# Second feed-forward stage of a fused attention and MoE kernel: three passes of 768 tokens, with the up products by Strassen's scheme

## The chip, the cores and the metric

The kernel runs on one core of a Trainium2 chip. The metric is the device time of one execution in microseconds (us). All operands of matmuls are 32-bit; a float that needs full precision is split into a high and a low part (both rounded for the matmul), and one product is made of three matmuls: high by high, high by low, low by high.

## The reference

Three stages follow each other: a random-feature attention, a feed-forward layer with a leaky activation (called MoE1 here), and four experts weighted by token (the second stage). The attention is left out; the rest is:

```python
def _moe_ref(x, w_in, w_out, alpha):            # x: 2304 x 512, w_in: 512 x 2048
    h = x @ w_in
    g = np.maximum(h, 0.0) + alpha * np.minimum(h, 0.0)
    return (g @ w_out).astype(np.float32)

def _moe2_ref(x, domain_probs, w1, w2):         # w1: 4 x 512 x 1024, w2: 4 x 1024 x 512
    p = domain_probs / (domain_probs.sum(-1, keepdims=True) + 1e-09)
    out = np.zeros((N, D), dtype=np.float32)
    for e in range(E):
        h = np.maximum(x @ w1[e], 0.0)
        out += p[:, e:e + 1] * (h @ w2[e])
    return out.astype(np.float32)
```

## The kernel before, in words

Tokens lie along the free axis of `Xh` and `Xl` (high and low part of a stage's input, 128 partitions x 4 blocks of 128 model columns x 2304 tokens). The 2304 tokens are five blocks: four of 512, one of 256. The hidden units of both feed-forward stages are cut in chunks of 128: chunks 0 to 15 are MoE1, chunks 16 to 47 the four experts. Four chunks make a group.

The attention and the first blocks of MoE1's first group run in an order that a planner (class `Plan`) fixed; from there on the code's own order holds. The loop over `steps` goes through groups, and within a group through the five token blocks. For one chunk and block, `up` makes 12 matmuls into a PSUM bank (`up_products`, L208), then the activation: in the second stage ACT writes the relu's high part `gh` (L219) and DVE the low part `gl` (L220). `down` makes 48 matmuls for a block of four chunks (`down_chunk`, L234), and `add` lays them into an accumulator in SBUF, in the second stage with the expert's probability as a factor (L268 to L275); the last group writes to `out`. The first up of the next step stands ahead of a step's down products, so that PE does not wait for the activations.

At the end of MoE1 `add` takes the finished block and splits it at once into `Xh` and `Xl`, the second stage's input (L259 to L262).

Weights: `fetch` loads a chunk's half (0 up, 1 down) from DRAM into one of five `raw` buffers. In the second stage that is one DMA of 256 KB from `wcat` on SP's queue (L186); `place` then splits it (L158 for the high part on ACT, L161 for the low part on POOL) into one of six places for up and five for down. Weights are used by five blocks while they lie there.

Every engine works through its instructions in order, SP's queue of DMA issues included. The names below: `up` and `dn` are PSUM banks of up and down products, `whu`/`wlu` and `whd`/`wld` weights (high, low; up, down), `gh`/`gl` activations, `acc_a`/`acc_b` the accumulators.

Of the kernel before, what the change touches and what calls it, by code (L numbers as in the profile page):

```python
# [19 lines left out]
P = 128  # L20
# [9 lines left out]
NCH = NF1 + E * NF2  # L30
NG = NCH // GRP
# [6 lines left out]
HMAX = 320  # L38
NA = 3
# [91 lines left out]
def fused(ctx: ExitStack, tc: tile.TileContext, qT, kT, v_main, v_tail, w_phi, alpha, probs, w64, wcat, out):  # L131
# [3 lines left out]
    def cp(eng, o, i):  # L135
        (eng.copy if eng is nc.scalar else eng.tensor_copy)(o, i)

# [15 lines left out]
    acc_a = big.tile([P, NA, CC * BLK], F32, name="acc_a")  # L153
    acc = [acc_a[:, i] for i in range(NA)]

# [24 lines left out]
    def fetch(c, half, w, st, u):  # L180

        if c < NF1:
            nc.sync.dma_start(st, w64[c, half])
            rounded(st, w.bitcast(U32), u)
        else:
            nc.sync.dma_start(w, wcat[c - NF1, half])  # L186
        raw[c, half] = w
# [23 lines left out]
    def up(c, blk):  # L211
# [6 lines left out]
        if c >= NF1:  # L218
            nc.scalar.activation(gh, ps, AF.Relu)  # L219
            nc.vector.scalar_tensor_tensor(gl, ps, 0.0, f32(gh), ALU.max, ALU.subtract)  # L220
        else:
            t = tpool.tile([P, BLK], F32, name="t")[:, :bn]
            nc.vector.tensor_scalar(t, ps, 0.0, alpha_sb[:, c:c + 1], ALU.min, ALU.mult)
            nc.vector.scalar_tensor_tensor(t, ps, 0.0, t, ALU.max, ALU.add)  # L224
            split(t, gh, gl, nc.scalar, nc.vector)
        gs[c, blk] = gh, gl

    def down_chunk(c, blk, i, ps, start, stop):
        wh, wl = wts[c, 1]
        gh, gl = gs[c, blk]  # L230
        sl = slice(i * P, (i + 1) * P)
        for k, (w, g) in enumerate(((wh, gh), (wl, gh), (wh, gl))):
            a, b = (w[:, sl], g) if c < NF1 else (g[:, sl], w)
            nc.tensor.matmul(ps, a, b, start=start and k == 0, stop=stop and k == 2)  # L234
# [5 lines left out]
    def down(chunks, blk, parts_):  # L240

        bn = BLOCKS[blk][1] if chunks[0] < NF1 else DM
        out_ps = [ps_d.tile([P, BLK], F32, name="dn")[:, :bn] for _ in parts_]
        for c in chunks:
            for i, ps in zip(parts_, out_ps):
                down_chunk(c, blk, i, ps, c == chunks[0], c == chunks[-1])
        for i, ps in zip(parts_, out_ps):
            add(chunks, blk, i, ps)

    def add(chunks, blk, i, ps):  # L250
        t0, bn = BLOCKS[blk]
        if chunks[0] < NF1:
            av = acc[blk][:, i * bn:(i + 1) * bn]
            if chunks[0] == 0:
                nc.vector.tensor_copy(av, ps)
            elif chunks[-1] < NF1 - 1:
                nc.vector.tensor_tensor(av, ps, av, ALU.add)
            else:
# [5 lines left out]
        tok = t0 // P + i  # L264
        av = acc[blk][:, i * DM:(i + 1) * DM]
        e = (chunks[0] - NF1) // NF2
        pe = pr[:, tok, e:e + 1]
        if chunks[0] == NF1:  # L268
            nc.vector.tensor_scalar_mul(av, ps, pe)
        elif chunks[-1] < NCH - 1:  # L270
            nc.vector.scalar_tensor_tensor(av, ps, pe, av, ALU.mult, ALU.add)  # L271
        else:
            o = opool.tile([P, DM], F32, name="o")
            nc.vector.scalar_tensor_tensor(o, ps, pe, av, ALU.mult, ALU.add)
            nc.sync.dma_start(out[tok * P:(tok + 1) * P], o)  # L275


    with ExitStack() as st1:
# [246 lines left out]
        for i in range(2):  # L525
            a = acc[1 + i].bitcast(U32)
# [179 lines left out]
```

## Time and profile before

| | us |
|---|---|
| median of three runs | 1438.38 |
| lowest and highest of them | 1437.92, 1438.8 |
| the profiled execution | 1439.93 |
| its span, first to last instruction | 1438.2 |
| PE busy in it | 1418.9 |
| DVE, ACT, POOL busy | 654.7, 412.4, 212.4 |

The span is what the trace covers; the profiled execution's own time has some 1.7 us more around it. Engines: PE is TensorE's matmuls (PEld its weight loads), DVE is VectorE, ACT ScalarE, POOL GpSimd, SP the engine that issues DMAs here. The matmuls are pipelined: the records of two neighbours overlap, so the pace is read from a row of many (its length over its count) and not from the length of one record.

### The profile page before, as it was taken

To read this page: it belongs to the slowest core of one execution; us is meant where nothing else is said; L and a number is where in the kernel's file an instruction comes from. 1 tells how busy PE (TensorE), PEld (TensorE's weight loads), DVE (VectorE), ACT (ScalarE), POOL (GpSimd) and SP (SyncE) were. 2 spreads that over 40 slices of the span, in tenths; PEclk is the share of its full clock that TensorE was granted. 3 is DMA by queue.
4 is the path that set the end of the run, shared out by engine and by line. 5 is a ranking of instruction groups with operands and counts; after the bars stand their busy time and mean duration, and the time that the engine had idled before them with its cause. 6 is when DMAs were issued, how large, how long until landed. Compare 5 with 4: busy or idle time off the path is not lost.

```text
span 1438.2 us, 17632 instructions
## 1 busy us (share of the span) xinstructions
PE 1418.9 (99%) x7200; PEld 1152.1 (80%) x7200; DVE 654.7 (46%) x1067; ACT 412.4 (29%) x857; POOL 212.4 (15%) x165
## 2 busy tenths in 40 slices
PE   7999999999999999999999999999999999999998
PEld 4667667778888888888888888888888888888887
DVE  7966656687958855663222222222222222222222
ACT  6877666632212112232021120121210201211110
POOL 3443223102002002011020020020100200200100
PEclk9999999999999999999999999999999999999999
DMA  4311111130202001001020020010100200100001
GB/s 148 112 50 51 50 50 51 53 103 30 88 1 59 30 8 52 1 23 37 0 59 0 1 59 0 8 52 1 30 30 0 59 0 8 52 0 0 30 30 74
DMA packets 25136, 53.67 MB, mean 37 GB/s; under 512 B 3168, under 2 KB 4320, under 8 KB 25056
## 3 DMA queue, kind: packets, MB, share of 16 engines
q1 hardware_dynamic: 25056, 52.55, 12.2%
q8 instruction: 57, 0.93, 0.3%
q14 instruction: 23, 0.19, 0.0%
HBM read 47.82 MB, written 4.72 MB: 37 GB/s over the span
## 4 chain that ended last, share of the span: by engine, by line
PE 94%; DVE 3%; ACT 1%; DMA 1%; issue 0%; SPq 0%; POOL 0%; ACTq 0%; DVEq 0%; POOLq 0%
PE up L208 39%; PE dn L234 39%; PE bank L437 4%; PE kv L379 3%; PE mm L208 2%; PE kv L385 2%; PE mm L234 2%; PE bank L420 1%; PE bank L348 1%; PE bank L349 1%; PE bank L350 1%; DMA st<-w 1%; DMA acc_a<-w 0%; PE bank L401 0%; DVE m L355 0%
## 5 line engine op out<-in xcount | busy, mean ns | idle before, releaser
L208 PE MATMUL up<-Xl,whu 128*128 128x512 f32 (+1 forms) x912 | 334.6, 367 | 0.0
L208 PE MATMUL up<-Xh,whu 128*128 128x512 f32 (+1 forms) x912 | 334.5, 367 | 0.0
L208 PE MATMUL up<-Xh,wlu 128*128 128x512 f32 (+1 forms) x912 | 334.4, 367 | 0.0
L219 ACT ACTIVATE gh<-up 128x512 fp32r<-128x512 f32 (+1 forms) x160 | 88.7, 555 | 539.5 <-PE up L208 539.4
L220 DVE SCALAR_TENSOR_TENSOR gl<-up,gh 128x512 fp32r<-128x512 f32 (+1 forms) x160 | 102.0, 638 | 303.8 <-ACT gh L219 303.7
L234 PE MATMUL dn<-whd,gh 128*128 128x512 f32 x576 | 224.2, 389 | 0.0
L234 PE MATMUL dn<-wld,gh 128*128 128x512 f32 x576 | 224.2, 389 | 0.0
L234 PE MATMUL dn<-whd,gl 128*128 128x512 f32 x576 | 224.1, 389 | 0.0
L208 PEld LDWEIGHTS up<-Xh,whu 128*128 128x128 f32 x912 | 172.0, 189 | 28.6
L208 PEld LDWEIGHTS up<-Xl,whu 128*128 128x128 f32 x912 | 172.0, 189 | 28.4
L208 PEld LDWEIGHTS up<-Xh,wlu 128*128 128x128 f32 x912 | 171.9, 189 | 28.2
L161 POOL TENSOR_TENSOR wlu<-w,whu 128x512 fp32r<-128x512 f32 x44 | 58.2, 1322 | 915.3 <-ACT whu L158 879.7
L234 PEld LDWEIGHTS dn<-whd,gl 128*128 128x128 f32 x576 | 108.1, 188 | 22.5
L234 PEld LDWEIGHTS dn<-whd,gh 128*128 128x128 f32 x576 | 108.2, 188 | 22.1
L234 PEld LDWEIGHTS dn<-wld,gh 128*128 128x128 f32 x576 | 108.2, 188 | 22.1
L271 DVE SCALAR_TENSOR_TENSOR acc_a<-dn,pr,acc_a 128x512 f32<-128x512 f32 x72 | 50.2, 751 | 135.4 <-PE dn L234 135.4
L234 PE MATMUL dn<-gh,wld 128*128 128x512 f32 (+1 forms) x272 | 99.1, 364 | 0.0
L234 PE MATMUL dn<-gh,whd 128*128 128x512 f32 (+1 forms) x272 | 99.1, 364 | 0.0
L234 PE MATMUL dn<-gl,whd 128*128 128x512 f32 (+1 forms) x272 | 99.0, 364 | 0.0
L158 ACT CAST gh<-t 128x512 fp32r<-128x512 f32 (+1 forms) x68 | 38.6, 569 | 134.8 <-DVE t L224 134.6
L437 PE MATMUL bank<-qe,kvt 128*128 128x256 f32 (+1 forms) x256 | 72.6, 417 | 0.9 <-DVE pmk L362 0.9
L158 ACT CAST whu<-w 128x512 fp32r<-128x512 f32 x44 | 27.3, 620 | 136.4 <-PE up L208 121.4
(121 smaller groups left out, 1734.8 us busy)
## 6 DMA issues: line engine op xcount, KB each, us to landing
w<-wcat SPq DMA_DIRECT2D x64, 256.0 KB, 2.6
st<-w SPq DMA_DIRECT2D x24, 512.0 KB, 3.5
kr<-kT SPq DMA_DIRECT2D x16, 288.0 KB, 2.8
qr<-qT SPq DMA_DIRECT2D x16, 288.0 KB, 2.8
out<-o SPq DMA_DIRECT2D x18, 256.0 KB, 2.0
v<-v_main SPq DMA_DIRECT2D x16, 256.0 KB, 3.0
acc_a<-w SPq DMA_DIRECT2D x8, 512.0 KB, 4.5
v<-v_tail SPq DMA_DIRECT2D x16, 32.0 KB, 2.9
```

The lines of the kernel that those rows point to most:

```text
L158: nc.scalar.copy(hi, src)
L161: lo_eng.tensor_tensor(lo, src, f32(hi), ALU.subtract)
L208: nc.tensor.matmul(ps[:, :bn], a[:, cs], x[:, cc, t0:t0 + bn], start=n == 0, stop=n == 3 * CC - 1)
L219: nc.scalar.activation(gh, ps, AF.Relu)
L220: nc.vector.scalar_tensor_tensor(gl, ps, 0.0, f32(gh), ALU.max, ALU.subtract)
L234: nc.tensor.matmul(ps, a, b, start=start and k == 0, stop=stop and k == 2)
L271: nc.vector.scalar_tensor_tensor(av, ps, pe, av, ALU.mult, ALU.add)
L348: nc.tensor.matmul(o, xh[:, tok], wbh, start=True, stop=False)
L349: nc.tensor.matmul(o, xh[:, tok], wbl, start=False, stop=False)
L379: nc.tensor.matmul(kv[h * D:(h + 1) * D, 0], v[:rows, tile_, h], e[:rows, 2 * i + h], start=tile_ == 0, stop=tile_ == len(TILES) - 1, skip ...
L385: nc.tensor.matmul(kv[r:r + 32, 1], ones[:rows], e[:rows, 2 * i + h], start=False, stop=tile_ + 2 >= len(TILES), tile_position=(0, r), ski ...
L437: nc.tensor.matmul(nd[:, :n], tl["kvt", p][:, 2 * h + s], tl["qe", (p, h, c)][:, s, :n], start=s == 0, stop=s == 1)
```

## The change

The second stage leaves the loop over `steps`, which keeps MoE1 only. It now runs in three passes of 768 tokens, each as two halves of 384, and in each pass over 16 pairs of chunks. With the model's 512 columns in two halves and a pair's 256 hidden units in two halves, one pair's up product is a 2 x 2 block product. It is computed by seven block products for eight, in Winograd's form of Strassen's scheme:

- Input sums. `inputs` makes four sums of quarters of MoE1's result (in place, in the accumulators) and splits the seven operands (`x_op`); they lie in `x7` and in six regions of `Xl` (`slots`). It runs once per pass.
- Weight sums. `weights_up`, in pass 0, loads a pair's four blocks in two DMAs of 256 KB (`wup`), makes four sums on POOL, splits the seven operands (ACT the high part, POOL the low), and writes each to DRAM (`wsu`), seven writes of 256 KB per pair. In passes 1 and 2 it only loads the seven. `weights_down` does the same for a chunk's down weights with one load (`wdn`) and two writes (`wsd`), and loads two per chunk later.
- Products. `up2` makes the seven products, each of 6 matmuls of 384 columns (L786), in three PSUM accumulators, `pb`, `pd` and `pa`. Two are copied out by ACT (p1, p5) before other products are added on top, a third (u1) in between; DVE adds these to accumulators for three of the four outputs (`total`, L799), and the fourth is read in place. Then relu and split as before, for 384 tokens (L793 on ACT, L794 on DVE).
- Down products. `down2` makes 36 matmuls of 512 columns for four chunks and 384 tokens, and adds them to `acc2` as before (L833, L842 to L844); in the last groups of a pass `acc2` goes to `out`.
- MoE1. Its finished blocks stay in the accumulators, now one tile of 4 x 1536 tokens and one of 4 x 768, and `add` no longer splits them. Buffers used by MoE1 alone (`stage`, `u`, `g`, `t`) moved behind the others and are released after it.

The diff, cut to its core:

```diff
-NCH = NF1 + E * NF2
-NG = NCH // GRP
+NG = NF1 // GRP
+BLK2 = 384
+NPASS = NT // (2 * BLK2)
+TB = BLK2 // P
+NPAIR = E * NF2 // 2
+SEQ = (1, 5, 6, 2, 7, 3, 4)
...
-    acc_a = big.tile([P, NA, CC * BLK], F32, name="acc_a")
+    acc = [big.tile([P, CC, NA * BLK], F32, name="acc_a")]
...
-            else:
-                ts = slice(t0, t0 + bn)
-                x = opool.tile([P, BLK], F32, name="o")[:, :bn]
-                nc.vector.tensor_tensor(x, ps, av, ALU.add)
-                split(x, Xh[:, i, ts], Xl[:, i, ts], nc.scalar, nc.vector)
-            return
...
+    slots = {k: Xl[:, :, i * BLK2:(i + 1) * BLK2] for i, k in enumerate((5, 6, 4, 2, 7, 3))}
+    slots[1] = x7
+    def x_op(k, src):
+        o = slots[k]
+        split(src, o[:, :2], o[:, 2:], nc.scalar, nc.vector)
+    def inputs(i, part):
+        a = lambda r, c: acc_of(slice(2 * c, 2 * c + 2), (2 * i + r) * BLK2, BLK2)
+        tt = nc.vector.tensor_tensor
+        if part == 0:
+            x_op(1, a(0, 0))
+            x_op(4, a(1, 1))
+            tt(a(1, 1), a(1, 0), a(1, 1), ALU.add)
+            x_op(5, a(1, 1))
+            tt(a(1, 0), a(1, 0), a(0, 0), ALU.subtract)
+            tt(a(0, 0), a(1, 1), a(0, 0), ALU.subtract)
+            x_op(6, a(0, 0))
+            x_op(2, a(0, 1))
+            tt(a(0, 1), a(0, 1), a(0, 0), ALU.subtract)
+        else:
+            x_op(7, a(1, 0))
+            x_op(3, a(0, 1))
...
+    def weights_up(i, f):
+        w = {k: up_place().rearrange("p (r c) -> p r c", r=2) for k in SEQ}
+        uw[i, f] = w
+        if i:
+            for j, k in enumerate(SEQ):
+                nc.sync.dma_start(f32(w[k]).rearrange("p r c -> p (r c)"), wsu[f][:, j])
+            return
...
+        def parts(k, src):
+            nc.scalar.copy(w[k][:, 0], src)
+            tt(w[k][:, 1], src, f32(w[k])[:, 0], ALU.subtract)
+            nc.sync.dma_start(wsu[f][:, SEQ.index(k)], f32(w[k]).rearrange("p r c -> p (r c)"))
+        parts(1, b[11])
+        tt(lo(5), b[12], b[11], ALU.subtract)
+        tt(lo(6), b[22], lo(5), ALU.subtract)
+        parts(5, lo(5))
+        tt(lo(4), b[21], lo(6), ALU.subtract)
+        parts(6, lo(6))
+        parts(2, b[21])
+        tt(lo(7), b[12], b[22], ALU.subtract)
+        parts(7, lo(7))
+        parts(3, b[22])
+        parts(4, lo(4))
+    def weights_down(i, c):
+        w = down_place()
+        dw[i, c] = w
+        if i:
+            for r in range(2):
+                nc.sync.dma_start(f32(w[r]), wsd[c][:, r])
+            return
+        t = raw_tile()
+        nc.sync.dma_start(t, wdn[c])
+        split(t, *w, nc.scalar, nc.vector)
+        for r in range(2):
+            nc.sync.dma_start(wsd[c][:, r], f32(w[r]))
...
+        product(1, "pb", True, False)
+        p1 = t("p1")
+        nc.scalar.copy(p1, ps["pb"])
+        product(5, "pd", True, False)
+        p5 = t("p5")
+        nc.scalar.copy(p5, ps["pd"])
+        product(6, "pb", False, False)
+        u1 = t("u1")
+        nc.scalar.copy(u1, ps["pb"])
+        product(2, "pa", True, True)
+        g(0, 0, total("pa", p1, "c11"))
+        product(7, "pb", False, False)
+        c22 = total("pb", p5, "c22")
+        product(3, "pd", False, True)
+        g(1, 0, total("pd", u1, "c12"))
+        product(4, "pb", False, True)
+        g(0, 1, ps["pb"])
+        g(1, 1, c22)
...
+    ups = [(i, f) for i in range(NPASS) for f in range(NPAIR)]
+    weights_up(0, 1)
+    for c in range(1, 4):
+        weights_down(0, c)
+    for n, (i, f) in enumerate(ups):
+        gp = f // 2
+        up2(i, f)
+        if n + 2 < len(ups):
+            weights_up(*ups[n + 2])
+        if f % 2 == 0:
+            if gp:
+                down2(i, gp - 1, 1, False)
+        else:
+            down2(i, gp, 0, False)
+            if n + 1 < len(ups):
+                i2, f2 = ups[n + 1]
+                for c in range(4):
+                    weights_down(i2, 2 * f2 + c)
+            if gp == NPAIR // 2 - 1:
+                down2(i, gp, 1, True)
+                if i + 1 < NPASS:
+                    inputs(i + 1, 0)
+                    inputs(i + 1, 1)
```

On PE, in the middle of the second stage, before: chunk after chunk of 12 matmuls, each by the high or low weights of that chunk (`whu`, `wlu`).

```order
L208 MATMUL up_8222<-Xh_75,whu_8131 128x512
L208 MATMUL up_8222<-Xl_76,whu_8131 128x512
L208 MATMUL up_8222<-Xh_75,wlu_8132 128x512 [waits Pool_49]
L208 MATMUL up_8222<-Xh_75,whu_8131 128x512
L208 MATMUL up_8222<-Xl_76,whu_8131 128x512
```

PE at the first pair of pass 0, after: the names `up_6340`, `up_6349` and `up_6366` are the accumulators pb, pd and pa; `whu`, `wlu` and `wx` are only places, each holding one operand's high and low part.

```order
L786 MATMUL up_6340<-x7_3540,whu_5816 128x384 x6
L786 MATMUL up_6349<-Xl_126,whu_5817 128x384 x6
L786 MATMUL up_6340<-Xl_126,wlu_5818 128x384 [waits Activation_49]
L786 MATMUL up_6340<-Xl_126,wlu_5818 128x384 x5
L786 MATMUL up_6366<-Xl_126,wlu_5819 128x384 x6
L786 MATMUL up_6340<-Xl_126,wx_5820 128x384 [waits Activation_49]
L786 MATMUL up_6340<-Xl_126,wx_5820 128x384 x5
L786 MATMUL up_6349<-Xl_126,wx_5821 128x384 x6
L786 MATMUL up_6340<-Xl_126,whu_5822 128x384 [waits DVE_49]
```

Where twelve matmuls of a bank stood, seven runs of six stand, and the third, fifth and seventh run wait for a read of the accumulator: p1's copy, u1's copy, and the total c22.

On ACT in the second stage, before: the relus of a group with the next weights' casts between them.

```order
L158 CAST whd<-w 128x512 x4
L219 ACTIVATE gh<-up 128x512 x15
L158 CAST whu<-w 128x512
L219 ACTIVATE gh<-up 128x256
L158 CAST whu<-w 128x512
```

On ACT in pass 0, after, around one pair's up products (p1, p5, u1 are the copies out of PSUM; `Xh_125` now holds relus and some down weights):

```order
L174 CAST Xh_125<-w_7885 128x512 [waits DMAHW2_49,PE_49]
L804 COPY p1_7727<-up_7720 128x384 [waits PE_49,Activation_49]
L695 CAST whu_7785<-w_7792 128x256 [waits DMAHW4_49]
L807 COPY p5_7736<-up_7729 128x384 [waits PE_49,Activation_49]
L695 CAST whu_7786<-ts0_7796 128x256 [waits DMAHW5_49,Pool_49]
L810 COPY u1_7744<-up_7720 128x384 [waits PE_49,Activation_49]
L695 CAST whu_7787<-ts1_7797 128x256 [waits DMAHW7_49,Pool_49]
L695 CAST wlu_7788<-w_7792 128x256 [waits DMAHW0_49,PE_49]
L793 ACTIVATE Xh_125<-c11_7753 128x384 [waits DVE_49]
```

The copies that PE waits for now stand between casts of weights, some of which wait for POOL (`ts0` and `ts1` are POOL's sums) or for a DMA.

On SP in the second stage, before: nothing but weight loads until the last group's writes.

```order
L186 DMA w_8333<-wcat 128x512 [waits DMAHW7_49,Pool_49]
L186 DMA w_8356<-wcat 128x512 [waits DMAHW0_49,Pool_49]
L186 DMA w_8379<-wcat 128x512 [waits DMAHW4_49,Pool_49]
L186 DMA w_8475<-wcat 128x512 [waits DMAHW5_49,Pool_49]
L186 DMA w_8494<-wcat 128x512 [waits DMAHW1_49,Pool_49]
```

On SP at the start of pass 0, after (`wsu1` and `wsd1` to `wsd3` are written, `w` from `wup` is a half of the third pair's raw weights):

```order
L687 DMA w_6412<-wup 128x512 [waits DMAHW2_49]
L697 DMA wsu1_58<-whu_6280 128x512 [waits DMAHW3_49,Pool_49]
L697 DMA wsu1_58<-wlu_6284 128x512 [waits DMAHW4_49,Pool_49]
L722 DMA wsd1_74<-whd_6316 128x512 [waits DMAHW5_49,Activation_49]
L722 DMA wsd1_74<-wld_6317 128x512 [waits DMAHW6_49,DVE_49]
L722 DMA wsd2_75<-whd_6324 128x512 [waits DMAHW7_49,Activation_49]
L722 DMA wsd2_75<-wld_6325 128x512 [waits DMAHW0_49,DVE_49]
L722 DMA wsd3_76<-whd_6332 128x512 [waits DMAHW1_49,Activation_49]
L722 DMA wsd3_76<-wld_6333 128x512 [waits DMAHW2_49,DVE_49]
L687 DMA w_6414<-wup 128x512 [waits DMAHW3_49]
```

The second half of the third pair's raw weights (`w_6414`) stands behind eight writes that wait for ACT, POOL or DVE.

## Rows read from the trace of the kernel before

**Rows 1.** the page: busy time, granted clock, GB/s by slice, and the chain's shares.

```profile
PE 1418.9 (99%) x7200; PEld 1152.1 (80%) x7200; DVE 654.7 (46%) x1067; ACT 412.4 (29%) x857; POOL 212.4 (15%) x165
...
PEclk9999999999999999999999999999999999999999
...
GB/s 148 112 50 51 50 50 51 53 103 30 88 1 59 30 8 52 1 23 37 0 59 0 1 59 0 8 52 1 30 30 0 59 0 8 52 0 0 30 30 74
...
PE 94%; DVE 3%; ACT 1%; DMA 1%; issue 0%; SPq 0%; POOL 0%; ACTq 0%; DVEq 0%; POOLq 0%
PE up L208 39%; PE dn L234 39%; PE bank L437 4%; PE kv L379 3%; PE mm L208 2%; PE kv L385 2%; PE mm L234 2%; PE bank L420 1%; PE bank L348 1%; PE bank L349 1%; PE bank L350 1%; DMA st<-w 1%; DMA acc_a<-w 0%; PE bank L401 0%; DVE m L355 0%
```

**Rows 2.** chain of waits piece by piece, second stage: start us, us, what.

```profile
645.08 5.75 PE dn L234 x48
...
749.14 10.88 PE up L208 x48
760.02 10.88 PE dn L234 x48
```

**Rows 3.** the end of the same chain.

```profile
1428.91 5.48 PE dn L234 x24
...
1434.41 0.75 DVE o L274
```

**Rows 4.** windows: us; PE, PEld, DVE, ACT, POOL busy; clock, DMA share, GB/s.

```profile
700.00:800.00 100.00, 100.00 (x466) 83.76 (x465) 26.05 (x39) 16.23 (x29) 10.33 (x8) 1.00 0.08 22
1350.00:1438.00 88.00, 84.38 (x395) 70.51 (x393) 22.76 (x34) 8.45 (x16) 0.00 (x0) 1.00 0.14 54
338.00:340.00 2.00, 2.00 (x11) 1.65 (x10) 0.00 (x0) 0.00 (x0) 0.00 (x0) 1.00 0.60 236
```

**Rows 5.** groups by form: operation, shapes, count; busy us, mean ns; idle before.

```profile
L234 PE MATMUL dn<-whd,gh 128*128 128x512 f32 x576 | 224.2, 389 | 0.0
...
L220 DVE SCALAR_TENSOR_TENSOR gl<-up,gh 128x512 fp32r<-128x512 f32 x128 | 88.5, 692 | 273.9 <-ACT gh L219 273.9
...
L219 ACT ACTIVATE gh<-up 128x512 fp32r<-128x512 f32 x128 | 76.6, 598 | 519.2 <-PE up L208 519.2
...
L161 POOL TENSOR_TENSOR wlu<-w,whu 128x512 fp32r<-128x512 f32 x44 | 58.2, 1322 | 915.3 <-ACT whu L158 879.7 <-DVE t L223 35.6
...
L271 DVE SCALAR_TENSOR_TENSOR acc_a<-dn,pr,acc_a 128x512 f32<-128x512 f32 x72 | 50.2, 751 | 135.4 <-PE dn L234 135.4
...
L161 DVE TENSOR_TENSOR gl<-t,gh 128x512 fp32r<-128x512 f32 x52 | 38.4, 738 | 25.8 <-ACT gh L158 25.5
...
L234 PE MATMUL mm<-gh,whd 128*128 128x512 f32 x48 | 19.2, 401 | 0.0
...
L220 DVE SCALAR_TENSOR_TENSOR gl<-up,gh 128x256 fp32r<-128x256 f32 x32 | 13.5, 424 | 29.8 <-ACT gh L219 29.8
...
L219 ACT ACTIVATE gh<-up 128x256 fp32r<-128x256 f32 x32 | 12.2, 381 | 20.3 <-PE up L208 20.3
```

**Rows 6.** timeline at two places: start us, us, engine, what, idle before.

```profile
299.96 0.68 DVE L565 SCALAR_TENSOR_TENSOR t<-mm,t 128x512 f32<-128x512 f32 x1
...
300.70 0.50 PE L208 MATMUL mm<-Xh,whu 128*128 128x512 f32 x1 [1.72 <-DVE t L565]
...
696.94 0.39 PE L208 MATMUL up<-Xh,whu 128*128 128x512 f32 x1
...
697.13 0.60 ACT L219 ACTIVATE gh<-up 128x512 fp32r<-128x512 f32 x1 [13.00 <-PE up L208]
```

**Rows 7.** DMA issues: KB each, median us from issue to landing.

```profile
w<-wcat SPq DMA_DIRECT2D x64, 256.0 KB, 2.6
st<-w SPq DMA_DIRECT2D x24, 512.0 KB, 3.5
...
out<-o SPq DMA_DIRECT2D x18, 256.0 KB, 2.0
```

**Rows 8.** waits of SP's queue: total us, times, longest us.

```profile
SPq L186 <- POOL wlu L161: 694.9, 32, 74.3
```

More of the change, by code (lines that the diff above doesn't have):

```diff
@@ new lines, in fused, with up_place, down_place @@
+    uw, dw = {}, {}
+    turn = [8, 0]
+    places = [(wa[0], "whu")] * 4 + [(wa[0], "wlu")] * 4 + [(wb[0], "whu")] * 2 + [(wb[0], "wlu")] * 2 + [(wx, "wx")] * 2
+    def up_place():
+        p_, name = places[turn[0] % len(places)]
+        turn[0] += 1
+        return p_.tile([P, DM], F32R, name=name)
+    XF = Xh.rearrange("p a b -> p (a b)")
+    def down_place():
+        at = turn[1] % 8
+        turn[1] += 1
+        if at < 5:
+            p_ = wa[1] if at < 4 else wb[1]
+            return [p_.tile([P, DM], F32R, name="w" + n + "d") for n in "hl"]
+        o = 16 * BLK2 + (at - 5) * 2 * DM
+        return [XF[:, o + r * DM:o + (r + 1) * DM] for r in range(2)]
@@ L668, in fused @@
             up(GRP * g2, b2)
-        n = CC if c0 < NF1 else BLOCKS[blk][1] // P
-        for d in ([[i] for i in range(n)] if last else [range(n)]):
-            down(range(c0, c1), blk, d)
+        else:
+            inputs(0, 1)
+        down(range(c0, c1), blk)
+        if c1 == NF1:
+            if blk == 1:
+                weights_up(0, 0)
+                weights_down(0, 0)
+            elif blk == 2:
+                inputs(0, 0)
+    st2.close()
+    apool = pool("acc2", 2)
+    tpool = pool("t2", 1)
@@ new lines, in fused, with up2, product, g @@
+    acc2 = {}
+    free = [XF[:, o:o + 2 * BLK2] for o in range(0, 16 * BLK2, 2 * BLK2)]
+    def up2(i, f):
+        ps = {k: None for k in ("pa", "pb", "pd")}
+        t = lambda name: tpool.tile([P, BLK2], F32, name=name)
+        w = uw.pop((i, f))
+        def product(k, name, start, stop):
+            if start:
+                ps[name] = ps_u.tile([P, BLK], F32, name="up")[:, :BLK2]
+            n = 0
+            for kt in range(2):
+                for r, x in ((0, 0), (0, 2), (1, 0)):
+                    nc.tensor.matmul(ps[name], w[k][:, r, kt * P:(kt + 1) * P], slots[k][:, x + kt],
+                                     start=start and n == 0, stop=stop and n == 5, skip_group_check=True)
+                    n += 1
+        def g(c, r, src):
+            o = free.pop(0)
+            gh, gl = (o[:, j * BLK2:(j + 1) * BLK2] for j in range(2))
+            nc.scalar.activation(gh, src, AF.Relu)
+            nc.vector.scalar_tensor_tensor(gl, src, 0.0, f32(gh), ALU.max, ALU.subtract)
+            gs[2 * f + c, r] = gh, gl, o
+        def total(name, x, out):
+            o = t(out)
+            nc.vector.tensor_tensor(o, ps[name], x, ALU.add)
+            return o
+        product(1, "pb", True, False)
[16 more added lines that the diff above has]
+        g(1, 1, c22)
@@ new lines, in down2, with product, add2 @@
+    def down2(i, gp, r, by_tile):
+        chunks = range(4 * gp, 4 * gp + 4)
+        ps = {}
+        def product(c, m):
+            if c == chunks[0]:
+                ps[m] = ps_d.tile([P, BLK], F32, name="dn")
+            gh, gl, _ = gs[c, r]
+            wh, wl = dw[i, c]
+            sl = slice(m * P, (m + 1) * P)
+            for k, (w, x) in enumerate(((wh, gh), (wl, gh), (wh, gl))):
+                nc.tensor.matmul(ps[m], x[:, sl], w, start=c == chunks[0] and k == 0, stop=c == chunks[-1] and k == 2)
+        def add2(m):
+            tok = (2 * i + r) * TB + m
+            if (gp, r, m) == (0, 0, 0):
+                acc2[i] = apool.tile([P, 2 * TB, DM], F32, name="acc2")
+            av = acc2[i][:, r * TB + m]
+            pe = pr[:, tok, 2 * gp // EP:2 * gp // EP + 1]
+            if gp == 0:
+                nc.vector.tensor_scalar_mul(av, ps[m], pe)
+            else:
+                nc.vector.scalar_tensor_tensor(av, ps[m], pe, av, ALU.mult, ALU.add)
+            if gp == NPAIR // 2 - 1:
+                nc.sync.dma_start(out[tok * P:(tok + 1) * P], av)
+        if by_tile:
+            for m in range(TB):
+                for c in chunks:
+                    product(c, m)
+                add2(m)
+        else:
+            for c in chunks:
+                for m in range(TB):
+                    product(c, m)
+            for m in range(TB):
+                add2(m)
+        for c in chunks:
+            free.append(gs.pop((c, r))[2])
```

128 lines of the change are left out of this document (65 added, 63 removed).

## The prediction

> **What bounds the kernel now.** I read the page first. PE is busy 99% of the span, its granted clock is at full speed in all forty slices, the chain that ended last is PE for 94%, and lines L208 (the up products of both feed-forward stages) and L234 (the down products) hold 39% each [rows 1]. The chain piece by piece then shows that the second stage, from about 645 us to 1434.4 us, is one unbroken row of PE pieces, up and down in turn, each beginning where the last ended [rows 2]. Nothing is waited for there, so its length is the number of matmuls times their pace: 10.88 us for 48 of 512 columns, which is 226.7 ns each, and 5.75 us for 48 of 256 columns, 119.8 ns each [rows 2]. Behind the last matmul only an add of 0.75 us and the last write are left [rows 3]. The windows give the rest: in 700 to 800 us ACT is busy for 16 of 100 us, DVE for 26, POOL for 10, and the DMA share is 0.08 [rows 4]. So the change takes time from the only full engine and gives work to four that are nearly idle. The question is whether any of them then makes PE wait.
>
> **What PE loses.** The up products of the second stage are now 32 chunks, each with 12 matmuls on four blocks of 512 tokens and one of 256: 384 x (4 x 226.7 + 119.8) ns = 394.2 us. After the change they are 3 passes x 16 pairs of chunks x 7 products x 6 matmuls = 2016, each of 384 columns. No row has 384. I take the middle of 256 and 512, 173.2 ns, since the two pieces fit a straight line (106.9 ns for 256 columns more, so 13 ns of fixed cost): 349.2 us. The saving is **44.9 us**, not the eighth of 49 us that the count alone promises, because shorter matmuls pay the fixed 13 ns more often. The weight loads beside PE run under matmuls of 119.8 ns without slowing them [rows 2], so 173 ns leaves them room. The pace has a worse bound: in stage one 48 down products have a mean record of 401 ns where the steady ones have 389 [rows 5]; 12 ns on 2016 matmuls would be +24 us. I take none of it, because the steady rows are those of this stage, with operands from the same memories.
>
> The Trainium skill (TensorE: Matmul & The Clock Gate, "Back-to-back issue gap") puts warm matmuls at N/2.4 ns plus about 2.5 ns. By that the saving would be about 45.8 us, an estimate from the page. The rows show 13 ns over N/2.4 at both widths, so the measurement decides, and the difference is under 1 us.
>
> The down products are 1728 matmuls of 512 before and after, at the same 226.7 ns: **0**. The tail, an add and a write, is the same: **0**. A pair of chunks then takes 42 x 173.2 ns = 7.28 us of up and 36 x 226.7 ns = 8.16 us of down, 15.44 us in all. All side work has to fit that.
>
> **Inside a pair.** The seven products share three accumulators, so the fifth product and later ones wait for copies and totals read out of them. Count from the pair's first matmul; a product lasts 1.04 us. From the last matmul's start to ACT's is 0.19 us beyond its slot, and ACT 128x256 takes 381 ns, 128x512 598 ns [rows 5, 6], so about 490 ns for 384. The copy p1 runs from 1.23 to 1.72 us and is wanted at 2.08; u1 from 3.31 to 3.80, wanted at 4.16. The DVE total c22 starts at 5.39, takes 558 ns (middle of 424 and 692 [rows 5]), ends at 5.95, and the last product wants it at 6.24. From DVE's end to PE's start the trace shows 0.06 us [rows 6], so the smallest margin is **0.23 us**. All hold, in every pass, if ACT and DVE are free at that moment. In passes 1 and 2 they have nothing else near. In pass 0, ACT has 7 casts of 128x256 for weights and 2 of 128x512 for the down weights per pair, and they stand in the queue between p1, p5, u1 and the relus. Busy time is no trouble: ACT 4 x 0.49 + 3 x 0.47 + 7 x 0.38 + 2 x 0.60 = 7.2 us, DVE 4 + 3 operations of 0.56, two of 0.74 and three adds of 0.75 = 7.6 us, POOL 11 of 128x256 at 0.66 to 1.33 us (half of a 512's time, or all of it [rows 5]) = 7.3 to 14.6 us, of 15.44. A cast before p1 in every second pair ends some 0.4 us ahead of its need. For one matmul held per pair I book what the one held matmul in the trace lost, 0.11 us (0.50 for 0.39 [rows 6]): 16 x 0.11 = **+1.8 us**, with bounds 0 and 40 (2.5 us per pair, below).
>
> **Transfers.** In pass 0 each pair reads 4 blocks of 256 KB and writes 11 back: 3.93 MB in 15.44 us, 255 GB/s. Each read alone lands 2.6 us after issue and each write 2.0 [rows 7], but 512 KB lands in 3.5 [rows 7], 0.9 us for 256 KB more, so a queue that is kept full moves 290 GB/s, and the write-heavy window at the end gives 54 GB/s at a share of 0.14, 386 GB/s at full share [rows 4]. At those rates the pair's transfers take 11 to 13.5 us. Passes 1 and 2 only read, 11 blocks a pair, 187 GB/s, 9.9 us. Transfers at 0.60 share beside PE leave PE busy for all of the 2 us of a window [rows 4], so I book **0** for contention.
>
> A rule speaks against this. The Trainium skill (DMA: Bandwidth & Descriptors, "Bandwidth") asks for 1 MiB or more in one transfer to reach three quarters of the peak; here all are a quarter of that. If each transfer paid its fixed part alone, a pair would take 15 x 2.6 us = 39 us by the trace's own landing time; this is the fourth case below. The rows of 256 and 512 KB say that most of the fixed part overlaps.
>
> **At the start of pass 0.** SP issues in order. One half of the raw weights of the third pair is queued on SP behind eight writes of made weights, which wait for POOL and DVE. The switch comes at 648.1 us (645.08 + 5.75, less 2.72 us of the old first up products [rows 2]); I place that load near 651 us, an estimate from the writes ahead of it; the sums of that pair come late on POOL, their casts stand on ACT ahead of p1 and u1 of the second pair, and no down products lie between the first pair and the second. By the operation times above p1 is late by some 2.9 us and u1 by 1.9: **+4.7 us**, bounds 0 and 9. The longest wait of SP now is 74 us for POOL's wlu [rows 8]: being late costs nothing there only because weights are loaded many blocks ahead, and that cover is gone in this place.
>
> **At the two pass ends.** The new inputs are made by DVE and ACT while PE does the two down products of the last pair, 16.3 us. Eleven DVE operations of 768 columns (about 1.03 us, one and a half of a 128x512's 0.69 [rows 5]) and six adds end some 14.5 us after the last up product, so they just fit; one subtraction stands in DVE's queue ahead of the first pair's c22 and eats its margin: **+1.2 us each, +2.4**, bounds 0 and 8.
>
> **Handover and first feed-forward stage.** Buffers of stage one are reused by other pools, so the first weight load behind it waits for DVE and POOL where it waited for all. The last group of MoE1 gets DVE and ACT work for the inputs and POOL work for the first weights. By the operation times [rows 5] DVE has about 16.9 us to do in such a block of 21.8 us (two pieces of 10.88 [rows 2]). I book **0**, bounds -3 and +3.
>
> **Sum.** -44.9 + 1.8 + 4.7 + 2.4 = -36.0 us. The profiled run took 1439.93 us, its span 1438.2, some 1.7 us outside; the median of three runs is 1438.38. I subtract from the median: **1402 us**.
>
> **Rivals.**
> 1. PE stays the bound and the losses are of the size above, 1394 to 1414 us: the forecast, **0.62**. For it speak the idle shares [rows 4]; against it, that margins of 0.2 us were worked out and not seen.
> 2. Side work of pass 0 holds PE in each pair: ACT's in-order queue waits in a weight cast for POOL or for a load, and p1, u1 or a relu waits behind it. At 1 to 2.5 us for each of 16 pairs, and as much again at the starts, 1418 to 1437 us: **0.17**. For it: POOL's bound of 14.6 us is near 15.44.
> 3. c22 is late in all 48 pairs because a 384-wide total reads two sources slower, or because releases take longer than 0.06 us. At 0.2 to 0.5 us each, +10 to +24: 1412 to 1426 us: **0.12**. The same times come from a pace slower by half of those 12 ns.
> 4. Slower than before: the one queue of transfers does not deliver pass 0. The point of decision is 36.0/16 = 2.25 us per pair more, that is 3.93 MB in 17.7 us, 222 GB/s. At 200 GB/s a pair takes 19.7 us, and if passes 1 and 2 (2.88 MB) keep up, the kernel gains 16 x 4.2 = 68 us: about 1470 us. With each transfer alone 39 us a pair, far above. For it: 255 GB/s over 247 us stands nowhere in the trace, whose highest slice is 148 GB/s [rows 1]. Against it: 236 GB/s in a window at 0.60 share [rows 4]. **0.09**.
>
> That the change does not do what it says is left out: the order of its instructions shows 2016 matmuls of 384 columns in place of the old ones.
>
> **How the numbers follow.** The low end is the saving with no loss, 1438.4 - 44.9 = 1393. The high end takes in the third case and the upper bounds of the small terms, 1426. Left out are most of the second case (0.10) and the fourth (0.09). A measurement here tells about 0.2%, 3 us, from no change. Faster: cases 1 and 3 and nearly all of 2, 0.88; the same: the upper end of 2 and the crossing of 4, 0.03; slower: 0.09.
>
> **What would show it.** Up products of 384 columns at a pace of 173 ns; passes 1 and 2 of 247 us each without a PE gap inside a pair; pass 0 longer than they are by 5 to 8 us, most of it in its first two pairs with PE released by ACT; the DMA share in pass 0 near 0.7 to 0.85. I am wrong if PE waits in each pair of pass 0 and the releaser is ACT (case 2) or a transfer (case 4), if DVE's total releases PE in every pair (case 3), or if 384 columns cost over 180 ns.

## The result, and the profile after

The changed kernel takes 1413.18 us (median of four, 1412.67 to 1415.91) against 1438.27 for the kernel before: ratio 0.9829, interval 0.9812 to 0.9846. It is faster by 25 us where 36 were forecast; the time lies inside the range, and 11 us above the point. The profiled execution took 1413.24 us, its span 1411.5, so that spans can be compared: by them 26.7 us were gained, because the profiled execution of the kernel before (1439.93) was 1.7 us above its median.

The page, with the lines that answer to [rows 1]:

```profile
PE 1382.5 (98%) x7296; PEld 1171.5 (83%) x7296; DVE 774.2 (55%) x1288; ACT 510.3 (36%) x1114; POOL 273.6 (19%) x277
...
PEclk9999999999999999999999999999999999999999
...
GB/s 141 116 51 60 51 51 51 10 90 76 90 16 31 60 1 120 1 16 180 289 292 250 236 240 223 204 230 195 184 164 179 195 197 232 199 192 164 172 157 45
...
PE 91%; DMA 3%; DVE 2%; ACT 2%; POOL 1%; issue 1%; SPq 1%; ACTq 0%; DVEq 0%; POOLq 0%
```

PE is still the bound, but DMA, ACT and POOL have entered the chain, and PE's share of the span fell from 99% to 98%. The forty slices of the clock hide what follows: a slice is 35 us long.

The chain piece by piece in the third pass, which answers to [rows 2] (start us, us, what):

```profile
1220.75 8.20 PE dn L833 x36
1228.95 7.30 PE up L786 x42
```

A pair takes 15.50 us, where 15.44 were forecast: 42 up products of 384 columns at 173.8 ns (forecast 173.2), 36 down products at 227.8 (226.7 before). The pairs of the second and third pass read like this one, but for one whose up products took 7.44 us.

The starts of the three passes are the first products of the first pair, on PE's timeline (start us, us, engine, line, operation):

```profile
651.25 0.51 PE L786 MATMUL up<-x,whu 128*128 128x384 f32 x2
...
911.13 0.69 PE L786 MATMUL up<-x,whu 128*128 128x384 f32 x3
...
1159.48 0.69 PE L786 MATMUL up<-x,whu 128*128 128x384 f32 x3
```

The three passes are thus 259.9, 248.35 and 248.2 us long (the third to the end of the last down product, 1407.70 us). The first loses 11.7 us against the third. And the first product starts at 651.25 us where the switch was at 648.1 before: another 3.1 us lost ahead of the second stage.

What PE waited for, from the list of the whole span (total us, times, longest us):

```profile
PE kv L368 <- ACT ke L357: 9.1, 7, 2.8
PE up L786 <- ACT p L804: 5.2, 2, 2.7
...
PE up L786 <- ACT u L810: 1.9, 1, 1.9
```

The wait for `ke` is in the attention stage; before it was 6.0 us on the same operation:

```profile
PE kv L379 <- ACT ke L368: 6.0, 6, 2.3
```

The waits of L786 lie at the start of the first pass: two in its second pair (2.46 us for p1's copy, 1.87 for u1's) and one in its fourth (2.75 us for p1's copy), as the timeline of PE has them in brackets:

```profile
663.44 1.41 PE L786 MATMUL up<-Xl,whu 128*128 128x384 f32 x6 [2.46 <-ACT p L804]
...
668.32 3.93 PE L786 MATMUL up<-Xl,wlu 128*128 128x384 f32 x13 [1.87 <-ACT u L810]
...
701.68 1.96 PE L786 MATMUL up<-Xl,whu 128*128 128x384 f32 x6 [2.75 <-ACT p L804]
```

Windows there, and two of steady stretches behind it (us; PE, PEld, DVE, ACT, POOL busy; granted clock, DMA share, GB/s):

```profile
652.00:656.00 4.00, 4.00 (x25) 4.00 (x24) 1.01 (x2) 1.82 (x5) 0.74 (x1) 1.00 0.99 339
660.00:664.00 4.00, 1.54 (x9) 1.22 (x8) 3.15 (x4) 4.00 (x11) 3.98 (x5) 1.00 0.19 71
664.00:668.00 4.00, 2.45 (x10) 1.94 (x8) 0.56 (x1) 0.60 (x3) 3.84 (x6) 0.57 0.81 307
668.00:672.00 4.00, 3.68 (x13) 3.69 (x14) 1.30 (x2) 2.33 (x6) 3.92 (x7) 0.58 0.40 150
731.00:800.00 69.00, 69.00 (x352) 62.99 (x351) 34.41 (x55) 31.64 (x75) 39.30 (x48) 1.00 0.74 265
900.00:1150.00 250.00, 250.00 (x1257) 226.23 (x1256) 102.79 (x174) 61.27 (x120) 0.00 (x0) 1.00 0.61 192
```

First the transfers are full (share 0.99, 339 GB/s), then PE stands for 2.5 of 4 us, and then the matmuls that do run have a granted clock of 0.57 and 0.58, so much of that stretch is at the lower of the two levels (1.2 for 2.4 GHz). A second such place is at 700 us (a clock of 0.76 in 700 to 704 us, 0.81 in 704 to 708). From 731 us on PE is busy without a gap, at a DMA share of 0.74 and 265 GB/s, with ACT, DVE and POOL at half their time or so.

The chain from the switch to the second product that waited, the one for u1, shows how the hold arises (start us, us, what):

```profile
651.45 0.63 ACT whd L174
...
652.16 0.70 DVE wld L177
652.86 0.02 issue
652.87 0.32 SPq L722
653.19 0.05 issue
653.25 4.42 DMA w<-wup
657.66 0.02 issue
...
657.80 0.74 POOL ts L700
...
667.79 0.48 ACT u L810
668.27 0.04 issue
668.32 2.30 PE up L786 x6
```

A cast of down weights (`whd`) had to wait for MoE1's last down products, whose place it takes. DVE then makes the low part, and the writes of both parts stand on SP ahead of the third pair's raw load. That load goes out at 653.25 and lands 4.42 us later, where such a load took 2.6 [rows 7]. POOL's sums begin 6.5 us after the switch, ACT's casts follow, and the copy u1 of the second pair stands behind them. This is the mechanism that the prediction put at this place, and the two waits, 2.46 and 1.87 us, are near the 2.9 and 1.9 that it gave them.

The fourth pair is held in another way, which the prediction does not have:

```profile
692.85 0.70 POOL whu L696
...
693.56 0.32 SPq L697
...
694.92 4.32 DMA w<-wdn
...
699.60 0.32 ACT whd L174
...
701.16 0.48 ACT p L804
...
701.68 7.03 PE up L786 x30
```

Here ACT waits for raw down weights before a cast, and p1 stands behind that cast. The load left SP at 694.92 us, behind a write that had waited for POOL's low part until 693.55 us and behind two other loads, and landed 4.32 us later. The order on SP and a slow landing are both in this chain.

### The profile page after: what moved, and what is told of

It is laid out like the page before. It is cut to its first block, busy times and chain, and to the rows that moved or that the text cites. A ratio compares the mean times of both kernels' runs of the same rounds, so it can differ in the third digit from the quotient of the medians.

```text
span 1411.5 us, 19676 instructions
## 1 busy us (share of the span) xinstructions
PE 1382.5 (98%) x7296; PEld 1171.5 (83%) x7296; DVE 774.2 (55%) x1288; ACT 510.3 (36%) x1114; POOL 273.6 (19%) x277
## 4 chain that ended last, share of the span: by engine, by line
PE 91%; DMA 3%; DVE 2%; ACT 2%; POOL 1%; issue 1%; SPq 1%; ACTq 0%; DVEq 0%; POOLq 0%
PE dn L833 27%; PE up L786 23%; PE dn L242 12%; PE up L221 12%; PE bank L426 4%; PE kv L368 3%; PE kv L374 2%; PE mm L242 2%; PE mm L221 2%; PE bank L409 1%; PE bank L337 1%; DMA acc_a<-w 1%; PE bank L338 1%; PE bank L339 1%; DMA w<-wdn 1%
## 5 line engine op out<-in xcount | busy, mean ns | idle before, releaser
L833 PE MATMUL dn<-whd,Xh 128*128 128x512 f32 x720 | 231.4, 390 | 0.0
L844 DVE SCALAR_TENSOR_TENSOR acc<-dn,pr,acc 128x512 f32<-128x512 f32 x126 | 88.7, 749 | 185.9 <-PE dn L833 185.9
L786 PE MATMUL up<-Xl,wlu 128*128 128x384 f32 x864 | 161.6, 339 | 1.9 <-ACT u L810 1.9
L833 PEld LDWEIGHTS dn<-whd,Xh 128*128 128x128 f32 x720 | 135.1, 188 | 27.0
L786 PEld LDWEIGHTS up<-Xl,wlu 128*128 128x128 f32 x864 | 153.5, 191 | 2.9 <-ACT u L810 2.4
L833 PE MATMUL dn<-Xh 128*128 128x512 f32 x648 | 151.8, 389 | 0.0
L799 DVE TENSOR_TENSOR c<-up,p 128x384 f32<-128x384 f32 x96 | 53.5, 557 | 176.6 <-PE up L786 176.6
L833 PEld LDWEIGHTS dn<-Xh 128*128 128x128 f32 x648 | 121.6, 188 | 25.5
L833 PE MATMUL dn<-wld,Xh 128*128 128x512 f32 x360 | 140.8, 391 | 0.0
L786 PE MATMUL up<-Xl,whu 128*128 128x384 f32 x576 | 112.9, 336 | 5.2 <-ACT p L804 5.2
L786 PEld LDWEIGHTS up<-Xl,whu 128*128 128x128 f32 x576 | 101.6, 189 | 6.0 <-ACT p L804 6.0
L793 ACT ACTIVATE Xh<-c 128x384 fp32r<-128x384 f32 x144 | 75.6, 526 | 80.2 <-DVE c L799 80.1
L221 PE MATMUL up<-Xl,whu 128*128 128x512 f32 (+1 forms) x272 | 99.1, 364 | 0.0
L221 PE MATMUL up<-Xh,whu 128*128 128x512 f32 (+1 forms) x272 | 99.1, 364 | 0.0
L221 PE MATMUL up<-Xh,wlu 128*128 128x512 f32 (+1 forms) x272 | 99.0, 364 | 0.0
L794 DVE SCALAR_TENSOR_TENSOR Xh<-c,Xh 128x384 fp32r<-128x384 f32 x144 | 86.4, 601 | 9.7 <-ACT Xh L793 4.3
L833 PEld LDWEIGHTS dn<-wld,Xh 128*128 128x128 f32 x360 | 67.5, 188 | 13.1
```

The costliest lines, as they stand in the source:

```text
L221: nc.tensor.matmul(ps[:, :bn], a[:, cs], x[:, cc, t0:t0 + bn], start=n == 0, stop=n == 3 * CC - 1)
L786: nc.tensor.matmul(ps[name], w[k][:, r, kt * P:(kt + 1) * P], slots[k][:, x + kt], start=start and n == 0, stop=stop and n == 5, skip_grou ...
L793: nc.scalar.activation(gh, src, AF.Relu)
L794: nc.vector.scalar_tensor_tensor(gl, src, 0.0, f32(gh), ALU.max, ALU.subtract)
L799: nc.vector.tensor_tensor(o, ps[name], x, ALU.add)
L833: nc.tensor.matmul(ps[m], x[:, sl], w, start=c == chunks[0] and k == 0, stop=c == chunks[-1] and k == 2)
```

## The experiments

Two theories were held against each other for the start of the first pass. A: the order on SP, one load behind eight writes. B: the transfers themselves, which are full with the writes of the first pairs, so that loads land late wherever they stand. Pass lengths below are read as above, from the first product of one pass to that of the next.

**The loads moved ahead.**

```diff
     weights_up(0, 1)
+    ups_raw[2] = load_up(2)          # the two loads of weights_up(0, 2)
     for c in range(1, 4):
         weights_down(0, c)
```

> The two raw loads of the third pair are issued ahead of the down weights 1 to 3 and their writes; nothing is left out. Theory A (order): PE's 7.1 us of waits for p1 and u1 at the start of pass 0, and the stretches at the lower clock behind them (some 3.9 us), come from that one load standing on SP behind eight writes, so both waiting places go: 1402 to 1405 us. Theory B (full transfers): the 256 KB transfers themselves are late because the queue is full from 648 to 700 us, whatever the order: 1410 to 1414 us, with PE still waiting for p1 or u1.

Measured: 1410.39 us (1409.68 to 1411.77), ratio 0.9804, 0.9788 to 0.9821. The first pass took 257.2 us, 2.7 less than in the changed kernel. PE still waited 6.3 us:

```profile
PE up L792 <- ACT u L816: 4.1, 2, 2.4
PE up L792 <- ACT p L810: 2.2, 1, 2.2
```

The changed kernel's times (from 1412.67 us) lie above all of these, so this order is worth some 2.7 of the 11.7 us. Theory A, that this one load makes both waiting places, fell. That the order on SP plays no part otherwise is not shown: the writes of the next pairs still stand ahead of loads, and there are only five raw buffers, so that the down weights of chunks 2 and 3 were now loaded at 647.93 and 652.81 us, where in the changed kernel the loads of all four chunks had gone out by 562 us.

The clock in this run shows that the length of a wait does not decide by itself. A wait of 2.4 us (for u1, in the first window) left it at 1.00; one of 2.2 us (for p1, just ahead of the second) was followed by a mean of 0.72 over 6 us:

```profile
682.00:688.00 6.00, 3.75 (x21) 3.66 (x22) 2.80 (x5) 2.70 (x7) 3.42 (x5) 1.00 0.75 278
...
700.00:706.00 6.00, 5.83 (x24) 5.84 (x25) 3.27 (x5) 3.29 (x10) 4.07 (x6) 0.72 0.81 305
```

**No writes for the first three pairs.** They are made again at each pass's start.

```diff
-        if i:
+        if i and f >= 3:
...
-            nc.sync.dma_start(wsu[f][:, SEQ.index(k)], ...)
+            if f >= 3:
+                nc.sync.dma_start(wsu[f][:, SEQ.index(k)], ...)
```

and the same for the down weights of chunks 0 to 5.

> The sums and down weights of the first three pairs are not kept in DRAM: they are made again at the start of each pass, with no write of theirs. Order of the loads as in the changed kernel. Theory A: the third pair's load stands behind no writes, so the start is as good as with the loads moved: 1402 to 1406 us. Theory B (full transfers): the same gain here, but none where only the order is changed. Against both: the remaking at the starts of passes 1 and 2 holds p1 there, up to 5 us each, 1407 to 1416 us.

Measured: 1406.33 us (1404.81 to 1406.81), ratio 0.9776, 0.9761 to 0.9790. The first pass took 251.0 us, 8.9 less; the second 248.2, no longer for the remaking at its start. (The execution profiled is the fastest of the four; by the medians the kernel gains 6.9 us.) So it is the writes of the first pairs that hold the first pass. Both theories forecast this gain, so this run does not say whether they do it by their order or by their bytes. PE's waits at the start were down to these:

```profile
PE up L788 <- ACT p L806: 1.1, 2, 0.8
PE up L788 <- DVE c L801: 0.7, 2, 0.5
```

The stretch from 645 to 705 us side by side, first the changed kernel, then the loads moved, then without the writes (columns as in the windows above):

```profile
645.00:705.00 60.00, 52.93 (x275) 48.90 (x274) 30.19 (x48) 26.60 (x63) 35.66 (x44) 0.92 0.76 269
```

```profile
645.00:705.00 60.00, 53.68 (x293) 49.51 (x292) 31.59 (x50) 28.57 (x68) 37.89 (x47) 0.97 0.79 278
```

```profile
645.00:705.00 60.00, 58.18 (x317) 53.03 (x316) 35.41 (x56) 30.32 (x72) 44.54 (x52) 1.00 0.65 228
```

PE gains 5.3 us of busy time and, beside it, the clock, which stays at 1.00 with waits of 0.8 us and less.

**Half the bytes, all the writes.** On top of the edit before, pass 0 writes again for the first three pairs, as many times but half the bytes.

```diff
             if f >= 3:
                 nc.sync.dma_start(wsu[f][:, SEQ.index(k)], ...)
+            elif i == 0:
+                nc.sync.dma_start(wsu[f][:, SEQ.index(k), :2 * P], f32(w[k])[:, 1])
```

and the same for the down weights of chunks 0 to 5.

> As without the first three pairs' writes (they are made again in each pass), but pass 0 still issues those writes, as many, with the same waits, each of half the bytes (128 KB). The third pair's loads then stand about where they stand with the loads moved ahead. If the bytes in the transfers hold the first pairs: half the way from 257.2 us of pass 0 (loads moved, full writes) to 251.0 (no writes), 253 to 255 us, and a kernel time near 1408 to 1409. If the number of writes and their waits on SP hold them: 257 us, 1410 to 1411.

Measured: 1408.89 us (1407.52 to 1410.94), ratio 0.9793, 0.9779 to 0.9806; the first pass 253.9 us, inside the 253 to 255 that the bytes would give and 3.3 below the 257.2 of full writes with the loads moved. This points to the bytes, but it does not show them. By the medians the two runs differ by 1.5 us, and their times overlap (1407.52 to 1410.94 here, 1409.68 to 1411.77 there); the profiles that give the pass lengths are of the fastest execution here and of the slowest there. Some 1.6 of the 3.3 us (0.28 x 5.83) are the lower clock of the other run in 700 to 706 us, where it stayed at 1.00 in this one. And the order on SP is near that of the loads moved ahead, but not the same row by row. What is clear is that half the bytes still cost 2.6 us against no writes at all (1404.81 to 1406.81 us).

**The sums' writes issued by POOL.**

```diff
-            nc.sync.dma_start(wsu[f][:, SEQ.index(k)], ...)
+            nc.gpsimd.dma_start(wsu[f][:, SEQ.index(k)], ...)
```

> The seven writes of a pair's sums are issued by POOL, which makes the low parts, and no longer stand on SP ahead of loads; the bytes are the same. Theory B (full transfers): the loads of the first pairs are as late as now, 1409 to 1414 us or worse by what issuing costs POOL. Theory A (order on SP): loads go out when their buffer is free, 1404 to 1408 us.

Measured: 1421.92 us (1419.92 to 1422.77), ratio 0.9887, 0.9873 to 0.9900. The first pass took 265.9 us, longer than the changed kernel's, and it is not only the start: between 731 and 900 us PE stands for 7.2 us. Groups on POOL between 700 and 880 us show a cost of its own (busy us, mean ns of one, idle before):

```profile
L697 POOL DMA_DIRECT2D wsu<-wlu x34 | 18.9, 557 | 11.8 <-POOL wlu L696 11.8
```

An issue keeps POOL for 0.56 us, seven times a pair. The time lies above both stated ranges, though theory B had left room for what issuing costs POOL. So the run tells that SP was the better place, but it doesn't tell order from bytes: it adds a cause.

**Nothing kept in DRAM.** All weights are made again in all passes (the edit of the second experiment with a bound above all pairs).

> Nothing is kept in DRAM: the weights' sums and the split down weights are made again in all three passes, by ACT, POOL and DVE as in pass 0; the writes and the reads back are left out. Theory (the writes of the first pairs fill the transfers; ACT, POOL and DVE keep up by themselves): passes 1 and 2 stay at 248 us, pass 0 at 250 to 251 as without the first writes: 1403 to 1408 us. Rival (casts between the copies hold p1 or u1 in each pair): 0.5 us or more for each of 32 pairs, over 1420 us. Beside it: if transfers are what makes 36 down products take 8.20 us and not 8.16, they take 8.16 in passes 1 and 2.

Measured: 1406.93 us (1405.42 to 1408.69), ratio 0.9785, 0.9771 to 0.9798. The passes took 249.9, 249.5 and 249.6 us. With ACT's casts and POOL's sums in every pair of every pass, PE lost about 1.3 us a pass, at a DMA share of 0.24:

```profile
900.00:1150.00 250.00, 249.30 (x1252) 225.24 (x1251) 135.21 (x204) 114.44 (x263) 147.32 (x176) 1.00 0.24 75
```

So the side work of ACT, POOL and DVE is hidden, as the working by pairs had it, and keeping the sums in DRAM costs more than it saves here: the writes of the first pairs cost some 9 us, the remaking in later passes 2.6. The 36 down products still take 8.20 us in those passes, at a DMA share of 0.24 where it was 0.61, so this much of the transfers is not why.

**The landing areas in one piece.** Back to stage one. The accumulator's new shape cut the areas in which MoE1's first weights land, 4 KB per partition for each load, into two pieces.

```diff
-            a = acc[0].bitcast(U32)[:, :, (1 + i) * BLK:(2 + i) * BLK]
-            areas.append([a[:, :2], a[:, 2].rearrange(...), a[:, 3].rearrange(...)])
+            a = acc[0].bitcast(U32)[:, 2 * i:2 * i + 2, BLK:3 * BLK]
+            cut = lambda x: x.rearrange("p (a b) -> p a b", a=2)
+            areas.append([cut(a[:, 0]), cut(a[:, 1, :BLK]), cut(a[:, 1, BLK:])])
```

The copies of MoE1's later blocks into that memory then wait for all eight of these weights, not for seven.

> The stage-one landing areas of the first weights lie in one piece of 4 KB per partition again, as before the change, in place of two pieces of 2 KB. Theory A: the 3.1 us that PE waits longer in stage one (9.1 for 6.0 us behind ACT's ke) come from these eight loads, which take SP 0.58 us to issue for 0.41: 1410 us. Rival: the difference is of another origin (another order of buffers or chance): 1413 us.

Measured: 1409.36 us (1408.48 to 1411.21), ratio 0.9800, 0.9786 to 0.9815; the first product of the second stage starts at 648.5 us, within 0.4 of the kernel before. The issues on SP (min/median/max ns) in the kernel before, in the changed one and with areas in one piece, and PE's wait with areas in one piece:

```profile
L536 SPq DMA_DIRECT2D acc_a<-w x8: 327/408/586, 4.5 to 52.9; - x8
```

```profile
L525 SPq DMA_DIRECT2D acc_a<-w x8: 551/578/612, 4.5 to 53.8; - x8
```

```profile
L526 SPq DMA_DIRECT2D acc_a<-w x8: 328/406/586, 4.5 to 53.2; - x8
```

```profile
PE kv L368 <- ACT ke L357: 5.1, 6, 1.5
```

The 3.1 us in stage one were these loads: the issue time is back at before's, and the wait for `ke` fell from 9.1 to 5.1 us. One profile alone would not carry this, since the start of the second stage differs by 2 us and more between profiles. But in all seven profiles with areas in two pieces it lies at 651.0 to 654.7 us, and in all four with areas in one piece at 646.1 to 648.5. Whether the longer issue or the later landing (a median of 5.1 us in two pieces, 4.5 in one) held PE was not told apart.

**An eighth product.**

```diff
         product(4, "pb", False, True)
+        product(1, "px", True, True)
```

> An eighth product of six matmuls, whose result nobody reads, is added to each pair; the output stays. Theory A (PE bounds every pair of every pass): 48 x 6 x 173.8 ns = 50.1 us more, less a few at the start: 1458 to 1464 us, and so slower than the kernel before by some 22 us: three passes with eight products would lose. Rival (pass 0 is bound by ACT, POOL or transfers): pass 0 absorbs its 16.7 us, 1445 to 1448 us.

Measured: 1467.39 us (1466.66 and 1468.12), ratio 1.0202, 1.0182 to 1.0223. In the third pass a pair's up products take 8.34 us for 7.30 and its down products the same 8.20:

```profile
1214.30 8.20 PE dn L834 x36
1222.51 8.34 PE up L786 x48
```

That is 50 us over 48 pairs, as worked out; the other 4 us, which put the time above both forecasts, lie ahead of the second stage (2.4 us, with a granted clock of 0.94 over the first 60 us for 0.97) and at the start of the first pass, where PE waited 9.3 us for p1. The first pass absorbed none of it, so it is bound by PE. It also shows what stands behind the gain: the same three passes, with all their sums and an eighth product, are 2% slower than the kernel before.

**The causes together.** Areas in one piece with nothing kept in DRAM:

> Landing areas in one piece and nothing kept in DRAM together. If the two causes add: 3.8 us less than the remaking alone, 1400 to 1404 us. If the remaking holds PE: over 1416 us.

Measured: 1401.24 us (1400.93 to 1402.12), ratio 0.9747, 0.9733 to 0.9760. Areas in one piece with the first three pairs not kept:

> Landing areas in one piece, and the first three pairs not kept in DRAM. If the two causes add: 1413.2 - 3.8 - 6.9 = 1402 to 1404 us.

Measured: 1399.91 us (1399.23 to 1400.25), ratio 0.9735, 0.9722 to 0.9748. The two causes add, and the time is 2 us better than forecast. Those 2 us lie ahead of the second stage, which starts at 646.55 us where it started at 648.50 with the areas alone; the granted clock in 10 to 20 us was 1.00 for 0.83, and what made this difference is open. Against 1401.24 us with nothing kept, whose times do not overlap, keeping the later pairs in DRAM is worth 1.3 us. And with the third pair's loads ahead as well:

> Landing areas in one piece, the first three pairs not kept, and the third pair's loads ahead of down weights 1 to 3. If the order of the loads still costs something without the writes ahead: 1397 to 1399 us. If not, the same 1400 us as without it.

Measured: 1399.65 us (1399.12 to 1401.26), ratio 0.9730, 0.9717 to 0.9743: no difference. Without writes ahead of them the order of these loads costs nothing. These last two beat both kernels, by 38 us the one before and by 13 us the changed one. The page of the one without the extra edit:

```profile
PE 1376.7 (98%) x7296; PEld 1167.0 (83%) x7296; DVE 790.4 (57%) x1300; ACT 529.7 (38%) x1168; POOL 333.8 (24%) x343
```

## Why the prediction was right, and where it was off

*Up products, -44.9 us.* Measured 48 x 7.30 = 350.4 us for 394.2, so -43.8. The middle between 256 and 512 columns was good to 0.6 ns a matmul. The bound of a slower pace was not needed. The 45.8 us given beside it go by a formula that the Trainium skill (TensorE: Matmul & The Clock Gate, "Back-to-back issue gap") states for a matmul by itself, and not for a row of many; the sum did not use it.

*Down products, 0.* Measured 48 x 8.20 = 393.6 us for 391.7: +1.9. A loss of 1.1 ns a matmul, seen in all passes, at a DMA share of 0.24 as at 0.61; its cause stays open.

*Inside a pair, +1.8 us.* Measured 0, or 0.1 in one pair: pairs of the first pass behind its start, and those of the second and third pass, take 15.50 us. (The first product that waits is the third, for p1, as the working's own 2.08 us has it, and not the fifth.) The margin of 0.23 us for c22 held, and the third case (late c22 in every pair) fell with it. The second case (side work in every pair) fell too, most clearly in the run that remakes all weights.

*Transfers, 0 for contention.* Right on the steady part: 265 GB/s at a share of 0.74 in 731 to 800 us, PE busy throughout; the share was forecast as 0.7 to 0.85. The rule of the Trainium skill (DMA: Bandwidth & Descriptors, "Bandwidth") that transfers want 1 MiB did not decide: 339 GB/s were moved in pieces of 256 KB (at a share of 0.99), with several under way at once. (At 386 GB/s a pair's 3.93 MB take 10.2 us and not 11; nothing hangs on it.) The fourth case, slower than before, rested on the queue failing over the whole pass and did not come.

*Start of the first pass, +4.7 us, bounds 0 and 9.* This is the step that failed in size: measured 11.7 us, above the bound. Place, mechanism and price of the first hold were right. The raw load behind eight writes went out 2.0 us after the switch (forecast 2.9), and p1 and u1 of the second pair, behind ACT's casts, were late by 2.46 and 1.87 us (forecast 2.9 and 1.9), 4.3 us together. The load had been given its undisturbed landing time, 2.6 us, and took 4.42; but these waits were not longer than forecast for it.

Two things were left out. The term ends with that hold, but loads stayed late: in the fourth pair p1 was held for another 2.75 us, by down weights whose load left SP behind a write and took 4.32 us to land. The mean need of 255 GB/s was set against the rate of a full queue, while the first pairs' transfers come in bursts: a share of 0.99 in 652 to 656 us, 0.19 in 660 to 664. And the clock was given no price, but it fell behind the waits of 2.46 and 2.75 us. In 664 to 672 us that is 0.43 x 2.45 + 0.42 x 3.68 = 2.6 us, by the clock of those windows, and some 1.3 us more between 700 and 708 us. The 7.1 us of waits and 3.9 of clock are 11.0 of the 11.7 us. That the writes of the first three pairs make the loads late is shown: without them 8.9 us come back. Whether by their bytes or by their order on SP stays open; the run with half the bytes points to the bytes.

*Pass ends, +2.4 us.* Measured 0.1 to 0.3 (the second and third pass against 16 x 15.50 us). The last split of the new inputs ended at 908.25 us, 2.9 us ahead of the first product of the second pass, so DVE was free when c22 came. The working took 1.03 us for an operation; they start 0.87 to 0.99 us apart. It also read the place of one subtraction in DVE's order as if it were reached late, which it was not.

*Handover and first stage, 0 with bounds -3 and +3.* Measured +3.1 by the two profiles, just outside, and not at the handover: the landing areas, at 4 to 54 us. The change names the accumulator's new shape, but the prediction did not follow it to the other users of that memory.

Sum by the profile: -43.8 + 1.9 + 11.7 + 3.1 and a few tenths in the second pass, some -27 us, against 26.7 between the two spans and 25.1 between the medians. With the start and the areas mended the kernel stands at 1399.9, near the 1402 that was forecast, but by another sum: what was booked as 8.9 us of losses is there some 2.8 us at the start and 1.9 of pace.

## What to carry to other kernels

A mean rate says little on the first trips of a loop that fills its buffers: work out the bytes and the landing times of the first three or four trips by themselves, with a landing time for a full queue, and do not stop at the first hold that is found. A wait of PE of some 2 us or more can have a second price, the clock behind it. Where side engines have half their time free, writing results to DRAM for later can cost more than making them again, if the writes fall on those crowded first trips; for the later trips keeping them still paid here, by 1.3 us. And when a tile's shape changes, follow every other user of its memory, in other stages too.

## What the runs showed of the hardware

- Loads of 256 KB that landed in 2.6 us (median) in the kernel before take 4.0 to 4.3 us (medians, 645 to 705 us) while the transfers are at a mean share of 0.76, and 4.42 us where the share is 0.99. The writes of the sums, also of 256 KB, landed in 2.0 to 2.1 us in that stretch, no later than the 2.0 of the writes to `out` before.
- A transfer of 512 KB whose landing is cut in two pieces per partition takes SP 578 ns to issue, in one piece 406 ns.
- POOL is busy for 557 ns with the issue of one transfer of 256 KB.
- After PE stood for 2.5 of 4 us the granted clock was 0.57 and 0.58 over the next 8 us, and 1.00 in the 4 us behind. With half the bytes, waits of 1.2 to 1.5 us left it at 1.00; with the loads moved ahead, a wait of 2.4 us left it at 1.00 and one of 2.2 did not.
- PE takes 1.1 ns longer for each down product after the change, with the same shapes, at a DMA share of 0.24 and of 0.61 alike; why is open.
